# Where the branch to the general path stands in a pooled-attention and mixture-of-experts kernel

## The chip, the cores and the metric

The kernel runs on one core of one Trainium2 chip. The metric is the time of one execution on the device, in microseconds (us); three runs of the kernel before took 638.83, 641.46 and 642.39 us, so the median is 641.46 us. Besides these there is one execution under the hardware profiler.

## What is computed

Attention with pooled keys and values makes 4608 rows of 512 numbers. A gate gives each row a score for each of 8 experts. Scores are taken from the highest down; a row goes to the expert of its best score that still has room (576 rows for each expert). Each expert then applies two matrices to its rows.

```python
def _moe_ref(x, w_gate, w1, w2):
    N, D = x.shape                     # 4608, 512
    E = w_gate.shape[1]                # 8
    cap = N // E                       # 576
    logits = x @ w_gate
    order = np.argsort(-logits.flatten())
    ...
    for idx in order:
        tok, e = int(idx) // E, int(idx) % E
        if assigned[tok] >= 0 or counts[e] >= cap:
            continue
        assigned[tok] = e
        counts[e] += 1
    ...
    for e in range(E):
        mask = assigned == e
        h = np.maximum(x[mask] @ w1[e], 0.0)
        out[mask] = h @ w2[e]
```

`x` is the output of the attention (8 batches, 8 heads, 576 positions, keys and values averaged over 8 neighbours).

## The kernel before

The program has three parts that follow each other. `Attention` works through 36 tiles of 128 rows, writes the rows to memory and collects the gate's scores. `Routing` then closes one expert at a time: a search for the threshold, a list of the 576 rows of this expert. `experts` runs the 8 experts one behind the other while the routing of the next one runs beside it.

An expert has two stages on TensorE (PE). Stage 1 (line 985) multiplies the gathered rows with `w1` in eight pieces of the hidden size, first for 256 columns and then for 320, twelve matmuls for each piece. ScalarE (ACT) applies the ReLU (lines 990, 992) and VectorE (DVE) makes the low part `hl` (line 993). Stage 2 makes five tiles of output. Tiles 0 to 3 take 24 matmuls each (line 1012); tile 4, with the last 64 rows, takes 16 matmuls in the program, which the trace shows as 32 (line 1023). Each tile goes from PSUM to SBUF on ACT (lines 1016, 1028) and from there to its rows in memory by an indirect DMA (a scatter) that GpSimd (POOL) issues (line 999), with a tiny MEMSET of `spacer` ahead of it. PSUM tiles named `h` rotate through five banks, the SBUF tiles `yt` through two.

The fast routing isn't exact in all cases. It adds up in `bad` whatever looks wrong, and `suspect` (lines 792 to 795) makes of it a `flag` by a DVE operation, a matmul with one column and another DVE operation. In the kernel before this stands in stage 2 of the last expert: `suspect` at step 24, and at step 48 each of the five engines loads the flag into a register (line 1225). After the last scatter stands a branch on the flag (line 1058), on every engine; SyncE (SP) only issues DMAs and waits. If the flag is set, `experts_one_by_one` does everything over again with an exact routing, in buffers of its own. If not, a short block follows that raises each engine's semaphores to what they would be after the skipped work: one count for PE, ACT and DVE, nine for SP, and on POOL one count and one instruction that raises the eight semaphores of its DMAs, behind waits for all earlier ones of these DMAs. Then comes the end of the program (line 1319): SP waits for all semaphores, every engine drains and meets the others twice, and POOL clears the semaphores. With the given data the flag isn't set.

The order in which the instructions of one engine stand is made when the program is built: Python generators yield after every matmul, and what is due goes in between. Behind stage 1 of the last expert nothing but stage 2, the branch and the end is left.

Of the kernel before, what the change touches and what calls it, by code (L numbers as in the profile page):

```python
# [883 lines left out]
class Experts:  # L884
# [4 lines left out]
    def __init__(self, tc, wk, psA, xd, w1, w2, out, ident, cap):  # L889
        self.tc, self.nc, self.wk, self.psA = tc, tc.nc, wk, psA  # L890
        self.xd, self.w1, self.w2, self.out, self.ident = xd, w1, w2, out, ident
        self.cap = cap
        self.scatters, self.raw1, self.raw2 = [], [], []
        self.spacer = wk.tile([1, 1], F32, name="spacer", bufs=1)

    @staticmethod
    def part(q):
# [8 lines left out]
    def load_1(self, eid, q0=0, q1=4):  # L906
        nc = self.nc
        r = nc.sync.value_load(eid[0:1, 0:1], min_val=0, max_val=7)
        if q0 == 0:
            self.raw1.append(self.wk.tile([128, 4, 1024], F32, name="raw1", bufs=1))  # L910
        src = self.w1[ds(r, 1)].rearrange("o (j p) f -> p (o j) f", p=128)
        for q in range(q0, q1):
            nc.sync.dma_start(self.raw1[-1][:, *self.part(q)], src[:, *self.part(q)])

    def load_2(self, eid):
        nc = self.nc
        r = nc.sync.value_load(eid[0:1, 0:1], min_val=0, max_val=7)
        raw = self.wk.tile([128, 8, 512], F32, name="raw2", bufs=1)
        src = self.w2[ds(r, 1)].rearrange("o (i p) d -> p (o i) d", p=128)
        for i in range(0, 8, 2):  # L920
            nc.sync.dma_start(raw[:, i:i + 2], src[:, i:i + 2])
        self.raw2.append(raw)

    def gather(self, rows):
        nc = self.nc
        self.xg = self.wk.tile([128, 5, 512], F32, name="xg", bufs=1)
        for t in range(5):
            n = min(128, self.cap - 128 * t)
            nc.gpsimd.indirect_dma_start(out=self.xg[:n, t, :], out_offset=None, in_=self.xd,  # L929
                                         in_offset=bass.IndirectOffsetOnAxis(ap=rows[:n, t:t + 1], axis=0))  # L930

    def high1(self, e, i):
        if i == 0:
            self.w1h = self.wk.tile([128, 4, 1024], F32R, name="w1h", bufs=1)
            self.w1l = self.wk.tile([128, 4, 1024], F32R, name="w1l", bufs=1)
# [6 lines left out]

    def high2(self, e, i):
        if i == 0:
            self.w2h = self.wk.tile([128, 8, 512], F32R, name="w2h", bufs=1)
            self.w2l = self.wk.tile([128, 8, 512], F32R, name="w2l", bufs=1)
        self.nc.scalar.activation(self.w2h[:, i], self.raw2[e][:, i], AF.Copy)

    def low2(self, e, i):
# [2 lines left out]
    def xt(self, t, name="tp", bufs=2, later=lambda after, t, f: f()):  # L952

        nc = self.nc
        n = min(128, self.cap - 128 * t)
        if t == 0:
            self.xh = self.wk.tile([128, 4, 576], F32R, name="xh", bufs=1)
            self.xl = self.wk.tile([128, 4, 576], F32R, name="xl", bufs=1)
# [8 lines left out]
    def stage1(self, later=lambda after, t, f: f(), halves=False):  # L967

        nc = self.nc
        hr = self.wk.tile([128, 8, 64], F32, name="hr", bufs=1)  # L970
        hh = self.wk.tile([128, 8, 576], F32R, name="hh", bufs=1)
        hl = self.wk.tile([128, 8, 576], F32R, name="hl", bufs=1)
        self.hr, self.hh, self.hl = hr, hh, hl
        cols = slice(0, 256), slice(256, 576)
        for o, some in ((cols[0], range(4)), (cols[1], range(4)), (cols[0], range(4, 8)), (cols[1], range(4, 8))) if (
                halves) else ((cols[0], range(8)), (cols[1], range(8))):
            m = o.stop - o.start
            dt = m / 2400 + 0.017
            for f in some:
                ps = self.psA.tile([128, 512], F32, name="h", bufs=5)  # L980
                n = 0
                for a, b in ((self.w1h, self.xh), (self.w1l, self.xh), (self.w1h, self.xl)):
                    for j in range(4):
                        fs = slice(128 * f, 128 * f + 128)
                        nc.tensor.matmul(ps[:, :m], a[:, j, fs], b[:, j, o], start=(n == 0), stop=(n == 11))  # L985
# [4 lines left out]
                nc.scalar.activation(hh[:, f, o], ps[:, :m], AF.Relu)  # L990
                if o.start:
                    nc.scalar.activation(hr[:, f], ps[:, 256:320], AF.Relu)  # L992
                later(0.65, 0.4, lambda f=f, o=o, m=m, ps=ps: nc.vector.scalar_tensor_tensor(  # L993
                    hl[:, f, o], ps[:, :m], 0.0, hh[:, f, o].bitcast(F32), op0=OP.max, op1=OP.subtract))
# [10 lines left out]
    def stage2(self, e, rows, halves):  # L1005
        nc = self.nc
        for t in range(4):
            ps = self.psA.tile([128, 512], F32, name="h", bufs=5)
            o = slice(128 * t, 128 * t + 128)
            for f in range(8):  # L1010
                for k, (a, b) in enumerate(((self.hh, self.w2h), (self.hl, self.w2h), (self.hh, self.w2l))):
                    nc.tensor.matmul(ps, a[:, f, o], b[:, f], start=(f == 0 and k == 0), stop=(f == 7 and k == 2))  # L1012
                    if f < 7 or k < 2:
                        yield 0.2275
            y = self.wk.tile([128, 512], F32, name="yt", bufs=2)
            nc.scalar.activation(y, ps, AF.Copy)  # L1016
            self.scatter(self.out, rows[:, t:t + 1], y)
            yield 0.2275

        ps = self.psA.tile([128, 512], F32, name="h", bufs=5)  # L1020
        for f in range(8):
            for a in range(2):
                nc.tensor.matmul(ps[64 * a:64 * a + 64, :256], self.hr[:, f], self.raw2[e][:, f, 256 * a:256 * a + 256],  # L1023
                                 start=(f == 0), stop=(f == 7))
            if f < 7:
                yield 0.44
        y = self.wk.tile([128, 256], F32, name="yh", bufs=2)
        nc.scalar.activation(y, ps[:, :256], AF.Copy)
        self.scatter(self.out.rearrange("n (a d) -> (n a) d", a=2), halves, y)
        yield 0.44  # L1030


@with_exitstack
def kernel(ctx, tc, q, k, v, wblk, moe_w1, moe_w2, out):
# [23 lines left out]
    with tc.If(flag > 0):  # L1058
# [4 lines left out]
def experts(ctx, tc, g, R, xd, w1, w2, out, ident, cap):  # L1063


    nc = tc.nc
# [129 lines left out]
    for e in range(8):  # L1196
# [5 lines left out]
        for n, dt in enumerate(X.stage1(later, not e)):  # L1202
# [9 lines left out]
                X.load_2(behind(1))  # L1212
            if n >= 64 and n % 2:
                w2.by((n - 70) // 14 if n > 70 else 0)
            advance(min(e + 1, 7), dt)
        while w2.l < 8:
            w2.next()
        w1 = pieces[e + 1] = Pieces(e + 1, X.high1, X.low1)
        for n, dt in enumerate(X.stage2(e, *toks[e])):
            advance(min(e + 1, 7), dt)  # L1220
            if not more and n == 24:
                assert next(g, None) is None
                flag = R.suspect()
            elif not more and n == 48:
                flag = nc.values_load(flag[0:1, 0:1], min_val=0, max_val=1)
            if more and due(e + 1, "id", 9):
                w1.by((n - 60) // 12 if n > 60 else 0)
            if more:
# [8 lines left out]
                turn(e + 1, t)  # L1237
        flush(2)
    flush()
    return flag  # L1240


def experts_one_by_one(ctx, tc, R, xd, w1, w2, out, ident, cap):

    nc = tc.nc
    wk = ctx.enter_context(tc.tile_pool(name="moe2", bufs=2))
    psB = ctx.enter_context(tc.tile_pool(name="psC", bufs=1, space=PSUM))
    X = Experts(tc, wk, psB, xd, w1, w2, out, ident, cap)
    R.restart()
    for e in range(8):  # L1250
        for step in R.exact(e):
# [10 lines left out]
            X.low2(e, i)  # L1262
        for t in range(5):
            X.xt(t)
        for _ in X.stage1():
# [57 lines left out]
```

## Time and profile before

| what | us |
|---|---|
| median of three runs | 641.46 |
| lowest and highest of the three | 638.83, 642.39 |
| the profiled execution, its own time | 640.09 |
| span from its first to its last instruction | 638.2 |
| outside the span, in that execution | 1.9 |
| PE busy in the span | 603.2 (95%) |
| start of the first matmul of stage 2 of the last expert | 598.98 |

The profile gives starts in us from the first instruction of the span. Busy time counts what an engine computes. Waits, branches and register loads belong to the engine's sequencer, which the views mark with a q behind the engine's name (POOLq); they aren't counted as busy, and are listed only by their source line. `PEld` is the loading of weights into PE.

### The profile page before, as it was taken

What the parts mean: (1) busy time and instruction counts of PE and PEld (TensorE: products, weight loads), DVE (VectorE), ACT (ScalarE), POOL (GpSimd) and SP (SyncE); (2) the same over time, 40 slices, a digit from 0 to 9 for tenths busy, and PEclk for the clock granted to TensorE, in tenths of its full rate; (3) what the DMA queues carried; (4) which work ended last, traced back from release to release, by engine and by line L of the source; (5) the groups of instructions that cost most, each with busy time, mean ns of one, the idle gap of its engine ahead of it and who ended that gap; (6) DMA issues with size and microseconds to landing.
All of it is one profiled execution on the core that took longest, in us unless ns stands there. A gap on an engine that the chain in (4) does not pass through costs nothing.

```text
span 638.2 us, 11819 instructions
## 1 busy us (share of the span) xinstructions
PE 603.2 (95%) x4516; PEld 522.3 (82%) x4516; DVE 396.9 (62%) x1142; ACT 244.1 (38%) x561; POOL 174.0 (27%) x215
## 2 busy tenths in 40 slices
PE   6999999994799999999999999999999999999991
PEld 3899998984598789779977987897799889879980
DVE  7677777888886768766862885386378236506100
ACT  6344444442362335233532433252345225415210
POOL 1999996000300410312111302120230213020011
PEclk9799999997799999999999999999999999999996
DMA  9989982121630743308103701630190054013010
GB/s 359 426 333 385 348 311 84 67 83 51 207 134 1 256 157 123 101 34 298 67 17 113 284 1 49 225 139 18 50 339 8 37 207 170 17 64 128 1 51 29
DMA packets 32578, 92.13 MB, mean 144 GB/s; under 512 B 3456, under 2 KB 3456, under 8 KB 29824
## 3 DMA queue, kind: packets, MB, share of 16 engines
q1 hardware_dynamic: 21296, 62.92, 26.5%
q0 software_dynamic: 5888, 18.88, 8.4%
q10 hardware_dynamic: 5328, 9.48, 3.9%
q8 instruction: 37, 0.61, 0.4%
q14 instruction: 29, 0.24, 0.1%
HBM read 72.40 MB, written 18.87 MB: 143 GB/s over the span
## 4 chain that ended last, share of the span: by engine, by line
PE 72%; issue 14%; DVE 7%; POOL 3%; DMA 2%; ACT 1%; POOLq 0%; SPq 0%; ACTq 0%; DVEq 0%
PE h L985 25%; PE h L1012 20%; PE psa L247 7%; PE pss L205 6%; PE h L1023 3%; PE tp L961 2%; PE pse L234 2%; POOL out_dram L999 1%; PE rt L234 1%; PE rt L195 1%; POOL xg L929 1%; PE rt L688 1%; PE rt L605 1%; PE rt L186 1%; PE rt L568 1%
## 5 line engine op out<-in xcount | busy, mean ns | idle before, releaser
L999 POOL DMA_INDIRECT out_dram<-yt,rows x32 | 33.2, 1036 | 280.5 <-ACT yt L1016 280.1
L1012 PE MATMUL h<-w2l,hh 128*128 128x512 f32 x256 | 102.8, 401 | 0.0
L1012 PE MATMUL h<-w2h,hl 128*128 128x512 f32 x256 | 102.0, 399 | 0.0
L1012 PE MATMUL h<-w2h,hh 128*128 128x512 f32 x256 | 101.2, 395 | 0.0
L985 PE MATMUL h<-xl,w1h 128*128 128x320 f32 (+1 forms) x512 | 95.9, 302 | 0.0
L985 PE MATMUL h<-xh,w1h 128*128 128x320 f32 (+1 forms) x512 | 91.2, 299 | 0.7 <-ACT xh L963 0.7
L985 PE MATMUL h<-xh,w1l 128*128 128x320 f32 (+1 forms) x512 | 91.7, 298 | 0.0
L990 ACT ACTIVATE hh<-h 128x320 fp32r<-128x320 f32 (+1 forms) x128 | 51.9, 409 | 99.1 <-PE h L985 96.9
L985 PEld LDWEIGHTS h<-xh,w1h 128*128 128x128 f32 x512 | 75.3, 189 | 3.6 <-issue 2.7
L985 PEld LDWEIGHTS h<-xl,w1h 128*128 128x128 f32 x512 | 77.0, 190 | 0.7
L985 PEld LDWEIGHTS h<-xh,w1l 128*128 128x128 f32 x512 | 76.1, 189 | 0.2
L965 DVE TENSOR_TENSOR xl<-tp,xh 128x512 fp32r<-128x512 f32 (+1 forms) x40 | 25.3, 633 | 78.7 <-ACT xh L963 78.4
L993 DVE SCALAR_TENSOR_TENSOR hl<-h,hh 128x320 fp32r<-128x320 f32 (+1 forms) x128 | 57.4, 451 | 25.3 <-ACT hr L992 16.3
L929 POOL DMA_INDIRECT xg<-xd,rows x40 | 39.7, 992 | 96.6 <-DVE rows L699 62.9
L1016 ACT ACTIVATE yt<-h 128x512 f32<-128x512 f32 x32 | 19.1, 597 | 119.7 <-PE h L1012 103.8
L247 PE MATMUL psa<-vblk,eT 128*128 128x146 f32 (+3 forms) x400 | 61.9, 303 | 0.0
L1012 PEld LDWEIGHTS h<-w2h,hl 128*128 128x128 f32 x256 | 48.1, 188 | 9.0
L1012 PEld LDWEIGHTS h<-w2l,hh 128*128 128x128 f32 x256 | 48.4, 189 | 8.2
L1012 PEld LDWEIGHTS h<-w2h,hh 128*128 128x128 f32 x256 | 48.2, 188 | 8.3
L247 PEld LDWEIGHTS psa<-vblk,eT 128*128 128x128 f32 (+1 forms) x400 | 52.2, 181 | 1.7 <-DVE xt L272 0.3
L205 PE MATMUL pss<-kblk,rawq 128*128 128x144 f32 (+1 forms) x320 | 45.9, 302 | 3.6 <-DVE e L216 2.8
L941 DVE TENSOR_TENSOR w1l<-raw,w1h 128x512 fp32r<-128x512 f32 x64 | 41.2, 686 | 8.1 <-ACT w1h L937 7.9
(194 smaller groups left out, 905.4 us busy)
## 6 DMA issues: line engine op xcount, KB each, us to landing
raw<-in_moe_w_dram SPq DMA_DIRECT2D x64, 512.0 KB, 6.8
xd<-xt ACTq DMA_DIRECT2D x36, 256.0 KB, 4.3
rawv<-in_v_dram SPq DMA_DIRECT2D x7, 1280.0 KB, 11.5
rawk<-in_k_dram SPq DMA_DIRECT2D x7, 1152.0 KB, 8.1
rawq<-in_q_dram SPq DMA_DIRECT2D x7, 1152.0 KB, 13.5
rawk<-in_k_dram SPq DMA_DIRECT2D x2, 576.0 KB, 4.6
rawv<-in_v_dram SPq DMA_DIRECT2D x1, 768.0 KB, 7.2
rawq<-in_q_dram SPq DMA_DIRECT2D x1, 640.0 KB, 8.7
```

The lines of the kernel that those rows point to most:

```text
L205: nc.tensor.matmul(ps[cols, j // 2, 144 * (j % 2):144 * (j % 2) + 144], self.q_of(b, j, n, cols.stop - cols.start), self.kblk[b % 4][:, j] ...
L234: nc.tensor.transpose(ps[:127, 128 * m:128 * m + 128], self.e[i][:, o:o + 127], self.ident)
L247: self.nc.tensor.matmul(o[h], self.eT[i][:, c, h], self.vblk[b % 4][:, self.BLOCKS[c]:self.BLOCKS[c + 1]], start=(c == cs[0]), stop=(c == ...
L929: nc.gpsimd.indirect_dma_start(out=self.xg[:n, t, :], out_offset=None, in_=self.xd, in_offset=bass.IndirectOffsetOnAxis(ap=rows[:n, t:t + ...
L941: self.nc.vector.tensor_tensor(l, raw, h.bitcast(F32), op=OP.subtract)
L965: later(1.3, 0.65, lambda: nc.vector.tensor_tensor(xl, ps[:, :, :n], xh, op=OP.subtract))
L985: nc.tensor.matmul(ps[:, :m], a[:, j, fs], b[:, j, o], start=(n == 0), stop=(n == 11))
L990: nc.scalar.activation(hh[:, f, o], ps[:, :m], AF.Relu)
L993: later(0.65, 0.4, lambda f=f, o=o, m=m, ps=ps: nc.vector.scalar_tensor_tensor(hl[:, f, o], ps[:, :m], 0.0, hh[:, f, o].bitcast(F32), op0= ...
L999: st = nc.gpsimd.indirect_dma_start(out=rows, out_offset=bass.IndirectOffsetOnAxis(ap=idx, axis=0), in_=y, in_offset=None)
L1012: nc.tensor.matmul(ps, a[:, f, o], b[:, f], start=(f == 0 and k == 0), stop=(f == 7 and k == 2))
L1023: nc.tensor.matmul(ps[64 * a:64 * a + 64, :256], self.hr[:, f], self.raw2[e][:, f, 256 * a:256 * a + 256], start=(f == 0), stop=(f == 7))
```

## The change

The branch moves from behind the last scatter to behind the products of the last expert's tile 1. Ahead of it stand now stage 1, tile 0 with its scatter, and the 24 matmuls of tile 1, whose sums stay in a PSUM bank. The branch follows. Behind it, for both paths, tile 1 is copied out and scattered and the tiles 2 to 4 are made. The general path therefore works in the same buffers as the fast one (`buf`, `fixed`) with two other PSUM banks (`bank`), and leaves out these last parts. The rows of the last expert are copied into `lastrows` (`keep`) so that both paths find them at one place. `suspect` and the load of the flag move into stage 1 of the last expert (steps 48 and 136).

```diff
-        flag = experts(c2, tc, g, R, xd, moe_w1, moe_w2, out, A.ident, cap)
-    with tc.If(flag > 0):
-        with ExitStack() as c2:
-            experts_one_by_one(c2, tc, R, xd, moe_w1, moe_w2, out, A.ident, cap)
+        rows = cst.tile([128, 6], I32, name="lastrows")
+        def keep():
+            nc.vector.tensor_copy(rows[:, :5], R.rows)
+            nc.vector.tensor_copy(rows[:, 5:], R.halves)
+        X, flag, ps = experts(c2, tc, g, R, xd, moe_w1, moe_w2, out, A.ident, cap, keep)
+        fast, X.scatters, X.fixed = X.scatters, [], True
+        with tc.If(flag > 0):
+            experts_one_by_one(X, R, ps)
+            keep()
+        X.scatters += fast
+        X.put(1, ps, rows, rows[:, 5:])
+        for _ in X.stage2(7, rows, rows[:, 5:], range(2, 5)):
+            pass
...
+            if not more and n == 48:
+                assert next(g, None) is None
+                flag = R.suspect()
+                keep()
+            elif not more and n == 136:
+                flag = nc.values_load(flag[0:1, 0:1], min_val=0, max_val=1)
             advance(min(e + 1, 7), dt)
...
-        for n, dt in enumerate(X.stage2(e, *toks[e])):
+        for n, dt in enumerate(X.stage2(e, *toks[e], range(5 if more else 1))):
             advance(min(e + 1, 7), dt)
-            if not more and n == 24:
-                assert next(g, None) is None
-                flag = R.suspect()
-            elif not more and n == 48:
-                flag = nc.values_load(flag[0:1, 0:1], min_val=0, max_val=1)
...
-    return flag
+    ps = psB.tile([128, 512], F32, name="h", bufs=5)
+    for _ in X.products(7, 1, ps):
+        pass
+    return X, flag, ps
...
+    def buf(self, name, shape, dtype=F32):
+        if not self.fixed:
+            self.bufs[name] = self.wk.tile(shape, dtype, name=name, bufs=1)
+        return self.bufs[name]
...
-        for _ in X.stage2(e, R.rows, R.halves):
+        for _ in X.stage2(e, R.rows, R.halves, range(5 if e < 7 else 1), bank):
             pass
+    for _ in X.products(7, 1, ps):
+        pass
```

`stage2` is split into `products` (the matmuls of a tile) and `put` (the copy and the scatter), which do what its body did before.

On PE, at the branch, the kernel before has the following; `hr` and `raw` belong to tile 4, and a name in brackets is the semaphore of an engine or a DMA that is waited for.

```order
L1012 MATMUL h<-w2l,hh 128x512
L1023 MATMUL h<-raw_7185,hr 64x256 [waits DMAHW4_49,Activation_49]
L1023 MATMUL h<-raw_7185,hr 64x256 x3
L1023 MATMUL h<-raw_7185,hr 64x256 [waits DMAHW5_49]
L1023 MATMUL h<-raw_7185,hr 64x256 x3
L1023 MATMUL h<-raw_7185,hr 64x256 [waits DMAHW6_49]
L1023 MATMUL h<-raw_7185,hr 64x256 x3
L1023 MATMUL h<-raw_7185,hr 64x256 [waits DMAHW7_49]
L1023 MATMUL h<-raw_7185,hr 64x256 x3
L1058 COMPARE_AND_BRANCH
```

On PE, where the two paths meet again in the changed kernel: the first row is the last matmul of the general path, the first branch leaves it, the second ends the short block of the fast path (its count waits for PE itself), and tile 2 follows.

```order
L1026 MATMUL h<-w2l,hh 128x512
L1081 UNCONDITIONAL_BRANCH
L1081 UNCONDITIONAL_BRANCH [waits PE_49]
L1026 MATMUL h<-w2h,hh 128x512 [waits DVE_49,Activation_49]
L1026 MATMUL h<-w2h,hl 128x512 [waits DVE_49]
L1026 MATMUL h<-w2l,hh 128x512
L1026 MATMUL h<-w2h,hh 128x512 [waits Activation_49]
```

Tile 4 stood ahead of the branch; now 64 matmuls of the program (tiles 2, 3 and 4) stand behind it, and the first of them stands behind a wait of PE for its own tile 1.

On POOL, at the branch, before: the scatters of tiles 1 to 4 stand ahead of it.

```order
L998 MEMSET spacer 1x1 [waits Pool_49]
L999 DMA out_dram<-yt,rows 4608x512 [waits DMASW5_49,Activation_49]
L998 MEMSET spacer 1x1 [waits Pool_49]
L999 DMA out_dram<-yt,rows 4608x512 [waits DMASW6_49,Activation_49]
L998 MEMSET spacer 1x1 [waits Pool_49]
L999 DMA out_dram<-yh,halves 9216x256 [waits DMASW7_49,DVE_49,Activation_49]
L1058 COMPARE_AND_BRANCH
```

On POOL, behind the branch, in the changed kernel: the row ISA is the instruction that raises the semaphores of the DMAs.

```order
L1081 UNCONDITIONAL_BRANCH
L1081 ISA [waits Pool_49,DMASW4_49,DMASW5_49,DMASW3_49,DMASW6_49,DMASW2_49,DMASW7_49,DMASW1_49,DMASW0_49]
L1081 UNCONDITIONAL_BRANCH
L1005 MEMSET spacer 1x1 [waits Pool_49]
L1006 DMA out_dram<-yt,lastrows 4608x512 [waits DMASW4_49,DVE_49,Activation_49]
L1005 MEMSET spacer 1x1 [waits Pool_49]
L1006 DMA out_dram<-yt,lastrows 4608x512 [waits DMASW5_49,Activation_49]
L1005 MEMSET spacer 1x1 [waits Pool_49]
L1006 DMA out_dram<-yt,lastrows 4608x512 [waits DMASW6_49,Activation_49]
L1005 MEMSET spacer 1x1 [waits Pool_49]
L1006 DMA out_dram<-yh,lastrows 9216x256 [waits DMASW7_49,DVE_49,Activation_49]
L1351 UNCONDITIONAL_BRANCH
```

Four scatters that stood ahead of this instruction now stand behind it, and between the last scatter and the end of the program stands nothing any more.

On ACT the copies of tiles 1 to 4 stand behind the branch, and the first of them waits for the semaphores of five DMAs of POOL.

```order
L1081 UNCONDITIONAL_BRANCH
L1081 UNCONDITIONAL_BRANCH [waits Activation_49]
L1040 ACTIVATE yt<-h 128x512 [waits DMASW3_49,DMASW2_49,DMASW4_49,DMASW0_49,DMASW6_49,PE_49,Activation_49]
L1040 ACTIVATE yt<-h 128x512 [waits DMASW3_49,DMASW5_49,DMASW1_49,DMASW7_49,PE_49,Activation_49]
L1040 ACTIVATE yt<-h 128x512 [waits DMASW4_49,PE_49,Activation_49]
L1044 ACTIVATE yh<-h 128x256 [waits PE_49]
```

Ahead of stage 1 of the last expert, all engines do the same in the same order as before.

More of the change, by code (lines that the diff above doesn't have):

```diff
@@ L925, in gather @@
         nc = self.nc
[L926 removed]
+        self.xg = self.buf("xg", [128, 5, 512])
         for t in range(5):
@@ L944, in high2 @@
         if i == 0:
-            self.w2h = self.wk.tile([128, 8, 512], F32R, name="w2h", bufs=1)
-            self.w2l = self.wk.tile([128, 8, 512], F32R, name="w2l", bufs=1)
+            self.w2h = self.buf("w2h", [128, 8, 512], F32R)
+            self.w2l = self.buf("w2l", [128, 8, 512], F32R)
         self.nc.scalar.activation(self.w2h[:, i], self.raw2[e][:, i], AF.Copy)
@@ L965, in xt, with stage1 @@
         later(1.3, 0.65, lambda: nc.vector.tensor_tensor(xl, ps[:, :, :n], xh, op=OP.subtract))
-    def stage1(self, later=lambda after, t, f: f(), halves=False):
+    def stage1(self, later=lambda after, t, f: f(), halves=False, bank=("h", 5)):
         nc = self.nc
-        hr = self.wk.tile([128, 8, 64], F32, name="hr", bufs=1)
-        hh = self.wk.tile([128, 8, 576], F32R, name="hh", bufs=1)
-        hl = self.wk.tile([128, 8, 576], F32R, name="hl", bufs=1)
+        hr = self.buf("hr", [128, 8, 64])
+        hh = self.buf("hh", [128, 8, 576], F32R)
+        hl = self.buf("hl", [128, 8, 576], F32R)
         self.hr, self.hh, self.hl = hr, hh, hl
@@ L979, in stage1 @@
             for f in some:
-                ps = self.psA.tile([128, 512], F32, name="h", bufs=5)
+                ps = self.psA.tile([128, 512], F32, name=bank[0], bufs=bank[1])
                 n = 0
@@ L1003, in scatter, with stage2, products @@
         self.scatters.append(st)
-    def stage2(self, e, rows, halves):
+    def stage2(self, e, rows, halves, parts=range(5), bank=("h", 5)):
+        for t in parts:
+            ps = self.psA.tile([128, 512], F32, name=bank[0], bufs=bank[1])
+            yield from self.products(e, t, ps)
+            self.put(t, ps, rows, halves)
+            yield 0.2275 if t < 4 else 0.44
+    def products(self, e, t, ps):
         nc = self.nc
[L1007 to L1010, printed above, removed]
+        o = slice(128 * t, 128 * t + 128)
+        for f in range(8):
+            if t < 4:
                 for k, (a, b) in enumerate(((self.hh, self.w2h), (self.hl, self.w2h), (self.hh, self.w2l))):
@@ L1014, in stage2, with put @@
                         yield 0.2275
+            else:
+                for a in range(2):
+                    nc.tensor.matmul(ps[64 * a:64 * a + 64, :256], self.hr[:, f],
+                                     self.raw2[e][:, f, 256 * a:256 * a + 256], start=(f == 0), stop=(f == 7))
+                if f < 7:
+                    yield 0.44
+    def put(self, t, ps, rows, halves):
+        if t < 4:
             y = self.wk.tile([128, 512], F32, name="yt", bufs=2)
-            nc.scalar.activation(y, ps, AF.Copy)
+            self.nc.scalar.activation(y, ps, AF.Copy)
             self.scatter(self.out, rows[:, t:t + 1], y)
[L1018 to L1030, printed above, removed]
+        else:
+            y = self.wk.tile([128, 256], F32, name="yh", bufs=2)
+            self.nc.scalar.activation(y, ps[:, :256], AF.Copy)
+            self.scatter(self.out.rearrange("n (a d) -> (n a) d", a=2), halves, y)
 @with_exitstack
```

25 lines of the change are left out of this document (12 added, 13 removed).

## Prediction

> **What bounds the kernel now.** First the page, for the span and the chain of work that ended last.
>
> ```profile
> span 638.2 us, 11819 instructions
> PE 72%; issue 14%; DVE 7%; POOL 3%; DMA 2%; ACT 1%; POOLq 0%; SPq 0%; ACTq 0%; DVEq 0%
> ```
>
> PE sets the pace nearly everywhere, and the edit touches PE only in the last expert. So the timeline of its last matmuls comes next, then the busy times of stretches behind them.
>
> ```profile
> 620.89 0.39 PE L1012 MATMUL h<-w2l,hh 128*128 128x512 f32 x1
> 621.21 3.67 PE L1023 MATMUL h<-raw,hr 128*64 128x256 f32 x32
> 624.93 0.38 ACT L1028 ACTIVATE yh<-h 128x256 f32<-128x256 f32 x1 [2.97 <-PE h L1023]
> 625.59 0.97 POOL L999 DMA_INDIRECT out_dram<-yh,halves  x1 [2.29 <-ACT yh L1028]
> ...
> 630.80:637.40 6.60, 0.00 (x0) 0.00 (x0) 0.00 (x0) 0.00 (x0) 0.00 (x0) 0.50 0.00 0
> 637.40:638.20 0.80, 0.00 (x0) 0.00 (x0) 0.00 (x0) 0.00 (x0) 0.00 (x0) 0.50 0.00 0
> ```
>
> PE is through at 621.21 + 3.67 = 624.9, the last scatter is issued by 626.6, and yet the span goes on to 638.2 with no engine computing and no DMA moving in its last 7.4 us. What happens there stands under the lines of the branch (1058) and of the program's end (1319), with the DMA view for the time that a scatter takes to land.
>
> ```profile
> L1058 SPq EVENT_SEMAPHORE  x9: 17/17/17, 608.3 to 608.9; - x9
> L1058 POOLq EVENT_SEMAPHORE  x5: 17/43/43, 628.0 to 628.9; - x5
> L1058 SPq COMPARE_BRANCH  x1: 53/53/53, 605.7 to 605.7; - x1
> L1058 PEldq COMPARE_BRANCH  x1: 3395/3395/3395, 622.6 to 622.6; - x1
> L1058 ACTq COMPARE_BRANCH  x1: 50/50/50, 624.9 to 624.9; - x1
> L1058 POOLq COMPARE_BRANCH  x1: 53/53/53, 625.4 to 625.4; - x1
> L1058 PEldq EVENT_SEMAPHORE  x1: 51/51/51, 626.0 to 626.0; - x1
> L1058 ACTq EVENT_SEMAPHORE  x1: 17/17/17, 627.5 to 627.5; - x1
> L1058 POOLq INC_SWDGE_SEM  x1: 1788/1788/1788, 628.9 to 628.9; - x1
> ...
> L1319 SPq EVENT_SEMAPHORE  x14: 17/28/28, 630.7 to 638.1; - x14
> L1319 POOLq DRAIN  x3: 40/107/6600, 630.8 to 637.9; - x3
> L1319 SPq DRAIN  x3: 7/7/13, 631.4 to 637.6; - x3
> ...
> out_dram<-yt,rows POOLq DMA_INDIRECT x4, 2.9
> out_dram<-yh,halves POOLq DMA_INDIRECT x1, 3.2
> ```
>
> Read as a chain: the last scatter lands at 625.59 + 3.2 = 628.8; POOL's waits for landed DMAs end there (628.9). INC_SWDGE_SEM, which raises the semaphores for the skipped DMAs, takes 1.79 us, to 630.7. POOL's first drain then takes 6.60 us, to 637.4, and the engines' last meeting 0.8. SP's twelve waits begin at 630.7 and its drains at 631.4, so SP is done 6 us before POOL. What bounds the end is the landing, the increments and the drain, in a row. The page's chain doesn't show it, since it ends with the last instruction that computes.
>
> **What goes from the end.** With the branch behind tile 1, the increments and the wait for their own scatter come four scatters earlier. Behind the last landing there remain SP's waits and the meeting: at most 631.4 - 630.7 = 0.7 us (the last scatter is the fourth of the twelve waits, so rather 0.5) and 0.8 us. The end would stand at 628.8 + 0.7 + 0.8 = 630.3 in place of 638.2: **7.9 us less**, as long as POOL's drain is short there. The same row's other two drains took 0.107 and 0.040 us; the long one is the one right behind INC_SWDGE_SEM. So I take the 6.6 us as work of that instruction which POOL finishes behind its record. The bounds of the drain at the new end are 0.04 and 6.60 us; I choose the lower, for the following rows.
>
> ```profile
> 605.56 0.97 POOL L999 DMA_INDIRECT out_dram<-yt,rows  x1 [31.44 <-ACT yt L1016]
> 606.53 0.09 POOL L998 MEMSET spacer<- 1x1 f32 x1
> ```
>
> The MEMSET starts when the scatter's 0.97 us are over: POOL has nothing left of a scatter after its record.
>
> **What the jump costs on PE.** Each engine that takes the branch is silent for some time: SP 605.7 to 608.3 (2.6 us), ACT 624.9 to 627.5 (2.6), POOL 625.4 to 628.0 (2.6), PE 622.6 to 626.0 (3.4, here inside the branch's own record). The DMA view tells what it waits for, in a window behind SP's and DVE's branches and one behind PE's:
>
> ```profile
> q14 instruction: 2, 0.02, 2.9%
> ...
> q8 instruction: 1, 0.02, 5.4%
> ```
>
> Two instruction pages in 1.75 us of 16 DMA engines (2.9%) are 0.4 us each; PE's single one in 1.1 us (5.4%) is 0.95 us. PE's jump is longer by about that difference, so its 3.4 us are a fetch, and not a wait for its matmuls, which ended at 624.9. The cover is PE's queue: the sequencer runs ahead of the array.
>
> ```profile
> L1023 PEldq EVENT_SEMAPHORE  x1: 51/51/51, 617.1 to 617.1; - x1
> 610.01 0.39 PE L1012 MATMUL h<-w2l,hh 128*128 128x512 f32 x1
> 610.24 0.39 PE L1012 MATMUL h<-w2h,hh 128*128 128x512 f32 x1
> 610.49 0.60 ACT L1016 ACTIVATE yt<-h 128x512 f32<-128x512 f32 x1 [5.20 <-PE h L1012]
> 598.83 0.19 PEld L1012 LDWEIGHTS h<-w2h,hh 128*128 128x128 f32 x1
> 598.98 0.39 PE L1012 MATMUL h<-w2h,hh 128*128 128x512 f32 x1
> ```
>
> The wait ahead of tile 4 was handled at 617.1, while the matmul just ahead of it started at 620.89: 3.8 us ahead, 17 matmuls of 0.23 us (610.24 - 610.01). Behind tile 1 stand the same matmuls, so the branch is taken 3.8 us before the last of them starts, and the 3.4 us fit in with 0.4 to spare. If that cover were gone, the jump would cost its 3.4 us. What stays open is the short block's wait for PE's own last product: the queue runs dry. From the start of the last matmul of tile 1 to the first of tile 2 I count 0.39 (the matmul), 0.09 (until its semaphore is seen: ACT starts 0.09 behind 610.01 + 0.39), two waits of 0.05, and 0.15 from weight load to matmul (598.83 to 598.98), less some overlap: 0.68. Normal is 0.23, so the **stall is 0.45 us**. Its bounds are 0.1 (620.89 to 621.21 at the change to tile 4, less 0.23) and 3.9 (the jump exposed, plus this).
>
> The Trainium skill bears on this, in "Runtime: NRT & Kernel Launch", section "Instruction fetch mechanics": a taken branch whose target isn't in the current two pages waits for a DMA that fetches the page, which speaks against a branch in the middle of PE's work. By that rule of the Trainium skill alone the sum would lose the whole jump, as in the second case of rival 1 below. The trace agrees that there is a fetch; that it lies behind queued matmuls is what the rows above add.
>
> **What is moved and added besides.** The flag's matmul had this price in stage 2:
>
> ```profile
> 604.44 0.39 PE L1012 MATMUL h<-w2h,hh 128*128 128x512 f32 x1
> 604.76 0.16 PE L794 MATMUL rt<-ones,rc 128*1 128x1 bf16 x1
> 605.19 0.40 PE L1012 MATMUL h<-w2l,hh 128*128 128x512 f32 x1
> ```
>
> From 604.44 to 605.19 one matmul of 0.23 lies between two, 0.75 for 0.46: it cost 0.3 us. In stage 1 it costs the like, so its move is 0, between -0.3 and +0.3. The loads of the flag stand in every engine's sequencer before and after; with PE's queue ahead they cost nothing. DVE gets two tiny copies and makes the flag ahead of one `hl`:
>
> ```profile
> 579.75 0.42 DVE L993 SCALAR_TENSOR_TENSOR hl<-h,hh 128x256 fp32r<-128x256 f32 x1 [1.02 <-ACT hh L990]
> 584.89 0.75 PE L985 MATMUL h<-xh,w1h 128*128 128x320 f32 x4
> ```
>
> DVE idles 1.02 us ahead of it. Waiting for the flag's matmul may push it back by some 0.4 us; its PSUM bank is next wanted, five banks on, at 584.89. That is 4.7 us of cover, so 0. Without it, each `hl` would hold PE by what it is late.
>
> The waits behind the branch need the scatters of tiles 1 and 2:
>
> ```profile
> 611.36 0.97 POOL L999 DMA_INDIRECT out_dram<-yt,rows  x1 [4.74 <-ACT yt L1016]
> 616.80 0.97 POOL L999 DMA_INDIRECT out_dram<-yt,rows  x1 [4.38 <-ACT yt L1016]
> ```
>
> Tile 0's scatter lands at 605.56 + 2.9 = 608.5, so the increments run from 608.5 to 610.3, hidden by tile 1's products. ACT's copy of tile 1 waits for them and for PE, as before at 610.5. On POOL, the 6.6 us behind the increments hold back tile 1's scatter until 610.3 + 6.6 = 616.9 in place of 611.4; behind it are queued tile 2's (ready at 616.8) and, one tile of 5.4 us later, tile 3's. Each takes 1.06 us with its MEMSET, so POOL is level again by 619.0. ACT's copy of tile 3 reuses tile 1's SBUF tile, which is free at 616.9 + 0.1 + 2.9 = 619.9, and wants it at 620.89 + 0.39 + 0.09 = 621.4. Both hide it, with 1.5 us to spare at least. Other engines have jumped by 608 and hold nobody.
>
> Sum: -7.9 + 0.45 + 0 = **-7.4 us**. The profiled execution took 640.09, span 638.2 and 1.9 around it; with the same 1.9 it becomes 632.7. It lies 1.4 below the median of the three runs and 0.6 below the mean of all four executions, 640.7, which I take as the level: **633.3**.
>
> **Rivals.**
> 1. *PE drains before it jumps on.* In the trace PE resumes at 626.0, 1.1 us behind its last matmul, and that could be a rule. For: no row shows a fetch that ended while matmuls were queued. Against: the lengths of the fetches above. The stall would be 0.39 + 1.1 + 0.3 - 0.23 = 1.6: -6.3, 634.4. With no cover at all it would be 3.9: -4.0, 636.7.
> 2. *The long drain belongs to the end*, whatever stands ahead of it, so the change doesn't bring what it says. For: one case only, at the end. Against: the MEMSET right behind the scatter, and no DMA was left to wait for. POOL then drains from 626.6 + 0.45 = 627.0 to 633.6, and 0.8: -3.8, 636.9.
> 3. *Slower: the 6.6 us move from the drain to each scatter behind the increments*, at POOL's queue (its state would have to be made good with every later DMA). The last issue would start at 610.3 + 4 x 6.6 + 3 x 1.06 = 639.9, and the end be at 639.9 + 3.2 + 1.5 = 644.6: +6.4, 647.1. It decides from 5.0 us a scatter (equal) and 5.8 (over 0.5%). Against: 0.97 us is a scatter's price everywhere in the trace, but no row shows one behind the increments.
>
> **How the numbers follow.** Forecast 0.70, rival 1 with 1.1 us 0.10, exposed 0.04, rival 2 0.12, rival 3 0.04. A measurement here tells 0.5%, 3.2 us, from no change. The forecast and rival 1 lie beyond it; rival 2, 3.8 below the level, falls inside half of the time. Faster 0.90, within 0.06, slower 0.04. The lower end: no stall (632.8) less 1.5 for the spread of executions (638.83 to 642.39): 631.3. The upper reaches rival 2 and the exposed jump: 637.2.
>
> **What would show it.** Right: a start-to-start gap near 0.7 us on PE between tiles 1 and 2; INC_SWDGE_SEM near 608.5; POOL's first drain at the end under 0.2 us; tile 1's scatter late, near 617; the span 630.8. A PE gap of 1.8 or 4 us is rival 1, a 6.6 us drain at the end rival 2, scatters 6 us apart rival 3. Wrong it would also be if something in stage 1 of the last expert came later by over 1 us.

## The result, and the profile after

The changed kernel takes **634.61 us**, the median of 14 executions (632.74 to 638.40), beside 640.74 of the kernel before (14 executions, 638.06 to 642.39). The ratio is 0.9924, with a 95% interval of 0.9901 to 0.9946: 4.9 us less, between 3.5 and 6.3. The forecast was 633.3 (631.3 to 637.2), and faster by over 0.5%. A second set of 12 executions gave 634.67 and 0.9923 (0.9893 to 0.9953). The time is near the forecast, but the profile shows that the main step of the forecast was wrong. The profiled execution took 637.23 us, with a span of 635.4; it is one of the longer of the 14.

First the timeline of the changed kernel's end, the counterpart of the rows of before that begin at 620.89 (start, duration, engine, line, operation).

```profile
622.31 0.39 PE L1026 MATMUL h<-w2l,hh 128*128 128x512 f32 x1
...
622.62 3.67 PE L1031 MATMUL h<-raw,hr 128*64 128x256 f32 x32
...
626.35 0.38 ACT L1044 ACTIVATE yh<-h 128x256 f32<-128x256 f32 x1 [2.97 <-PE h L1031]
627.00 0.97 POOL L1006 DMA_INDIRECT out_dram<-yh,lastrows  x1 [2.29 <-ACT yh L1044]
```

Then the stretches behind it (busy time of PE, PEld, DVE, ACT and POOL, then the clock, the DMA share and GB/s).

```profile
628.00:629.40 1.40, 0.00 (x0) 0.00 (x0) 0.00 (x0) 0.00 (x0) 0.00 (x0) 1.00 0.26 94
629.50:634.60 5.10, 0.00 (x0) 0.00 (x0) 0.00 (x0) 0.00 (x0) 0.00 (x0) 0.66 0.00 0
634.60:635.40 0.80, 0.00 (x0) 0.00 (x0) 0.00 (x0) 0.00 (x0) 0.00 (x0) 0.50 0.00 0
```

The last scatter has landed by 629.4, and there are still 5.1 us in which nothing computes and nothing moves. The instructions of the branch (line 1081 now) and of the program's end (1351) say who fills them: each row has count, shortest/median/longest in ns, and the start of the first and of the last.

```profile
L1081 POOLq EVENT_SEMAPHORE  x5: 17/43/1647, 609.2 to 611.1; - x5
L1081 SPq COMPARE_BRANCH  x1: 53/53/53, 581.2 to 581.2; - x1
L1081 DVEq COMPARE_BRANCH  x1: 72/72/72, 601.0 to 601.0; - x1
...
L1081 ACTq COMPARE_BRANCH  x1: 50/50/50, 605.9 to 605.9; - x1
L1081 POOLq COMPARE_BRANCH  x1: 53/53/53, 606.5 to 606.5; - x1
L1081 PEldq COMPARE_BRANCH  x1: 3942/3942/3942, 607.0 to 607.0; - x1
L1081 ACTq EVENT_SEMAPHORE  x1: 17/17/17, 608.5 to 608.5; - x1
L1081 POOLq INC_SWDGE_SEM  x1: 1708/1708/1708, 611.2 to 611.2; - x1
L1081 PEldq EVENT_SEMAPHORE  x1: 51/51/51, 611.3 to 611.3; - x1
...
L1351 POOLq DRAIN  x3: 40/113/7813, 626.8 to 635.2; - x3
L1351 SPq DRAIN  x3: 7/7/13, 630.0 to 634.9; - x3
```

The increments left the end, as meant: they run at 611.2 to 612.9. SP drains from 630.0, 0.6 us behind the landing. But **POOL's first drain is still there**. It is on record from 626.8, when POOL's sequencer reached it behind the last issue, and ends at 626.8 + 7.8 = 634.6: 6.6 us behind the end of the scatter's record at 627.0 + 0.97. In the kernel before it took 6.60 us directly behind the increments. From the start of the last scatter's issue to the end of the span there were 638.2 - 625.59 = 12.6 us; there are 635.4 - 627.00 = 8.4 now, where the forecast had 4.7.

In the middle of stage 2 the new wait looks as follows, on PE, POOL and ACT.

```profile
610.85 0.39 PE L1026 MATMUL h<-w2l,hh 128*128 128x512 f32 x1
611.53 0.47 PE L1026 MATMUL h<-w2h,hh 128*128 128x512 f32 x1 [0.30 <-PEq L1081]
...
612.98 0.09 POOL L1005 MEMSET spacer<- 1x1 f32 x1 [5.26 <-DMA out_dram<-yt,rows]
...
613.04 0.60 ACT L1040 ACTIVATE yt<-h 128x512 f32<-128x512 f32 x1 [6.57 <-DMA out_dram<-yt,rows]
...
613.92 0.97 POOL L1006 DMA_INDIRECT out_dram<-yt,lastrows  x1 [0.85 <-ACT yt L1040]
```

From the last matmul of tile 1 to the first of tile 2 are 0.68 us. POOL's MEMSET follows the increments at once, at 612.98, and tile 1's scatter starts at 613.92, not near 617.

### The profile page after: what moved, and what is told of

Its sections match the earlier page's. It is cut to its first block, busy times and chain, and to the rows that moved or that the text cites. A ratio compares the mean times of both kernels' runs of the same rounds, so it can differ in the third digit from the quotient of the medians.

```text
span 635.4 us, 11825 instructions
## 1 busy us (share of the span) xinstructions
PE 605.0 (95%) x4516; PEld 524.1 (82%) x4516; DVE 394.5 (62%) x1144; ACT 244.1 (38%) x561; POOL 174.8 (28%) x215
## 4 chain that ended last, share of the span: by engine, by line
issue 47%; PE 24%; POOL 14%; DMA 9%; DVE 4%; ACT 0%; POOLq 0%; SPq 0%; DVEq 0%; ACTq 0%
DMA out_dram<-yt,rows 7%; PE psa L247 6%; POOL xg L936 6%; POOL out_dram L1006 6%; PE pss L205 5%; PE h L992 5%; PE h L1026 2%; PE pse L234 2%; PE rt L234 1%; PE rt L195 1%; PE rt L186 1%; PE rt L568 1%; DMA rawk<-in_k_dram 1%; DMA xg<-xd,rows 1%; DMA raw<-in_moe_w_dram 1%
## 5 line engine op out<-in xcount | busy, mean ns | idle before, releaser
L1006 POOL DMA_INDIRECT out_dram<-yt,rows x29 | 30.3, 1046 | 262.1 <-ACT yt L1040 261.6
```

What stands on the lines that cost most here:

```text
L1006: st = nc.gpsimd.indirect_dma_start(out=rows, out_offset=bass.IndirectOffsetOnAxis(ap=idx, axis=0), in_=y, in_offset=None)
```

## The experiments

Software DMAs are here the gathers and scatters that POOL issues, 40 of each. Three theories stood at first. *A, a debt*: POOL's drain makes good something for each software DMA issued since the drain before, so it can be paid early. *B* and *C*: it has a fixed price, B at any drain, C at the program's end. Against all of them stood the forecast's own reason, that the time hangs on the increments.

**A drain in POOL's idle time** (mid_drain), a line in the loop over stage 1:

```diff
+            elif not more and n == 100:
+                nc.gpsimd.drain()
             elif not more and n == 136:
                 flag = nc.values_load(flag[0:1, 0:1], min_val=0, max_val=1)
```

> The changed kernel with one drain of POOL added in stage 1 of the last expert (n = 100), where POOL idles for some 20 us. 75 of the 80 software DMAs (40 gathers, 40 scatters) are ahead of it, 5 behind. Theory A, a debt: POOL's drain makes good something for every software DMA since the drain before, 6.6 / 80 = 0.083 us each. Then the added drain takes 6.2 us in POOL's idle time, the first one at the end 0.4 us; the end is set by the last scatter's landing and SP's waits, span 4.5 us shorter than the changed kernel's, time 630.1. Theory B, a fixed price of any drain behind POOL's DMAs: both take 6.6 us, time 634.6. Theory C, it belongs to the program's end: the added one under 0.2 us, the end's 6.6, time 634.6.

Measured: 629.10 us, ratio to before 0.9827 (0.9795 to 0.9859). The rows of the end, of the increments and of the added drain (line 1248):

```profile
L1353 POOLq DRAIN  x3: 46/113/2899, 623.0 to 626.8; - x3
L1353 SPq DRAIN  x3: 7/7/13, 626.2 to 626.5; - x3
...
L1081 POOLq INC_SWDGE_SEM  x1: 203/203/203, 607.3 to 607.3; - x1
...
L1248 POOLq DRAIN  x1: 9169/9169/9169, 570.0 to 570.0; - x1
```

and POOL's timeline around both drains:

```profile
570.19 0.97 POOL L1006 DMA_INDIRECT out_dram<-yh,halves  x1 [2.29 <-ACT yh L1044]
579.78 0.09 POOL L1005 MEMSET spacer<- 1x1 f32 x1 [8.62 <-issue]
...
623.22 0.97 POOL L1006 DMA_INDIRECT out_dram<-yh,lastrows  x1 [2.29 <-ACT yh L1044]
```

The added drain ends at 579.2, 8.0 us behind the issue ahead of it, while PE computes. The one at the end is over 1.7 us behind the last issue (623.0 + 2.9 = 625.9), and SP's drains at 626.2 end last. B and C are out; of A's numbers neither fits closely (6.2 and 0.4 us were expected, 8.0 and 1.7 measured). The increments, of which no expectation had spoken, shrank too: 0.20 us in place of 1.71.

**The same drain with the branch in its old place** (old_place_drain): the kernel before with the two added lines.

> The kernel before, with its branch at the end, and the same added drain in stage 1 of the last expert. It separates the drain from the branch's place. Theory A (debt): end drain 0.4 us, SP's waits and drains then end last, some 0.7 us behind the increments; span 638.2 - 6.6 + 0.7 = 632.3, time 634.8, as fast as the changed kernel without the branch moved. Theories B and C: no change, 640.7, end drain 6.6 us.

Measured: 633.79 us, ratio 0.9877 (0.9852 to 0.9903). This added drain alone is worth no less than the whole change.

```profile
L1321 POOLq DRAIN  x3: 46/107/463, 630.8 to 632.1; - x3
...
L1058 POOLq INC_SWDGE_SEM  x1: 288/288/288, 630.5 to 630.5; - x1
```

A long drain isn't tied to the increments ahead of it, nor to the program's end: here it stands right behind them and takes 0.46 us.

**The change without its branch** (no_branch):

```diff
-        with tc.If(flag > 0):
-            experts_one_by_one(X, R, ps)
-            keep()
```

> The changed kernel without its branch: the general path for tied or odd inputs is left out, as is the increment of the skipped DMAs' semaphores; the flag is still made and loaded. It shows what the branch still costs in its new place. If the jump is covered by PE's queue: the start-to-start gap of PE between tiles 1 and 2 falls from 0.68 us to 0.23-0.3, tile 4 ends 0.4 us earlier, POOL's end drain stays 6.6 us whatever the increments did (theories A, B and C alike). If the long drain hangs on the increments (my forecast's reason): end drain under 0.2 us and a span 4.9 us shorter than the changed kernel's.

Measured, in the rows of the end and on PE between tiles 1 and 2:

```profile
L1348 POOLq DRAIN  x3: 40/113/7813, 625.8 to 634.2; - x3
```

```profile
610.43 0.39 PE L1026 MATMUL h<-w2l,hh 128*128 128x512 f32 x1
610.66 0.39 PE L1026 MATMUL h<-w2h,hh 128*128 128x512 f32 x1
```

With no increments at all the drain is 7813 ns, to the nanosecond that of the changed kernel. And the start-to-start gap is 0.23 us: the branch costs PE 0.68 - 0.23 = 0.45 in its new place. By the end drain the forecast's own reason is out. The single time, 636.20, tells nothing at this size.

**How does the debt grow?** Five kernels vary the number of software DMAs since the last drain. eight_drains has the added line in every expert (`if n == 100:`), drain_expert3 and drain_expert1 in one (`if e == 3 and n == 100:` and 1). few_scatters adds none and leaves out the scatters of the first seven experts, and so their rows of the output:

```diff
-            self.put(t, ps, rows, halves)
+            self.put(t, ps, rows, halves, e == 7)
...
+            if out:
+                self.scatter(self.out, rows[:, t:t + 1], y)
```

drain_first is the kernel before with a drain ahead of its first gather.

> The changed kernel with a POOL drain in stage 1 of each of the eight experts (n = 100). Software DMAs ahead of each since the drain before: 5, 10, 10, 10, 10, 10, 10, 10, and 5 for the one at the end. Theory A (debt per DMA): 0.4, then seven times 0.8, end 0.4 us. Theory B (fixed): nine times 6.6 us. Theory C: eight times under 0.2, end 6.6. A debt that grows with POOL's other instructions (most of them in the first 110 us) rather than with its DMAs: the first long, the others short.

> The changed kernel with one added POOL drain, in stage 1 of the fourth expert: 40 software DMAs ahead of it, 40 behind. Theory A (debt per DMA, 6.61 / 80 = 0.083 us): the first drain at the end finishes 40 x 0.083 = 3.3 us behind the end of the last scatter's issue; if the debt is added to the 1.69 us that five DMAs left, it is 1.69 + 35 x (6.61 - 1.69) / 75 = 4.0. INC_SWDGE_SEM took 1.71 us with 76 DMAs since the last drain and 0.20 with one, so with 36 near 0.9. Theory D (only the first drain of a program is dear, as a code that must be brought in once): 1.69 us at the end as with the drain in the last expert, INC_SWDGE_SEM 0.2.

> The same with the drain in stage 1 of the second expert: 15 software DMAs ahead, 65 behind. Theory A: 65 x 0.083 = 5.4 us behind the end of the last scatter's issue (5.6 if added to the 1.69), INC_SWDGE_SEM 1.4 us with 61. Theory D: 1.69 and 0.2 us.

> The changed kernel without the scatters (and their MEMSETs) of the first seven experts; their rows of the output are left out. No drain is added; 45 software DMAs are left, 40 gathers and 5 scatters. Theory A (debt per DMA): end drain 45 x 0.083 = 3.7 us behind the end of the last issue (4.3 if added to 1.69), INC_SWDGE_SEM with 41 of them 1.0 us, in place of 1.71. Theory D or a debt in time or in POOL's other work: 6.6 us. A debt of scatters alone: 1.69 us; of gathers alone: 6.6 us.

> The kernel before, with a POOL drain ahead of its first software DMA: some 90 of POOL's own instructions ahead of it, no software DMA. Theory A (debt per DMA): it takes under 0.2 us, INC_SWDGE_SEM 1.8 and the first drain at the end 6.6 us as before; from the start of the last scatter to the span's end 12.6 us; time 640.7, ratio 1.000. A debt of POOL's other work would show here as a long drain. It is also the control for the runs' gains, which came out larger than what the ends of the traces account for (-4.9 for -3.7 us with the change, -11.1 for -8.2 with the drain in the last expert): if each build has an offset of its own, whatever is changed in it, the ratio here lies 0.2 to 0.4% away from 1.

Two of them in the rows of their ends, first drain_expert3 and then few_scatters, each with the last scatter from its timeline:

```profile
L1353 POOLq DRAIN  x3: 46/113/4543, 625.1 to 630.3; - x3
...
L1081 POOLq INC_SWDGE_SEM  x1: 908/908/908, 609.3 to 609.3; - x1
```

```profile
625.38 0.97 POOL L1006 DMA_INDIRECT out_dram<-yh,lastrows  x1 [2.29 <-ACT yh L1044]
```

```profile
L1353 POOLq DRAIN  x3: 40/113/4955, 623.8 to 629.3; - x3
...
L1083 POOLq INC_SWDGE_SEM  x1: 1004/1004/1004, 608.2 to 608.2; - x1
```

```profile
624.02 0.97 POOL L1006 DMA_INDIRECT out_dram<-yh,lastrows  x1 [2.29 <-ACT yh L1045]
```

The drain of drain_expert3 ends at 625.1 + 4.54 = 629.6, 3.3 us behind the end of the last issue; that of few_scatters 3.8 behind. The four kernels of this group that ran on the changed one took 631.07 (eight_drains), 632.34 (drain_expert3), 632.68 (drain_expert1) and 631.37 us (few_scatters) in one execution each, which is too few to order them. All kernels together, with branch_stage1 from below (the column "0.083 n" is 6.61 / 80 for each DMA, and 0.19 + 0.02 n a line through the increments of old_place_drain and of the kernel before; nothing else is fitted; tail runs from the start of the last scatter's issue to the end of the span):

| kernel | DMAs since the last drain, n | 0.083 n | end drain, behind the last issue | DMAs at the increments | 0.19 + 0.02 n | increments | tail |
|---|---|---|---|---|---|---|---|
| after | 80 | 6.6 | 6.6 | 76 | 1.71 | 1.71 | 8.4 |
| no_branch | 80 | 6.6 | 6.6 | none | - | - | 8.4 |
| branch_stage1 | 80 | 6.6 | 6.6 | 75 | 1.69 | 1.69 | 8.4 |
| drain_expert1 | 65 | 5.4 | 5.4 | 61 | 1.41 | 1.41 | 7.2 |
| few_scatters | 45 | 3.7 | 3.8 | 41 | 1.01 | 1.00 | 5.6 |
| drain_expert3 | 40 | 3.3 | 3.3 | 36 | 0.91 | 0.91 | 5.1 |
| mid_drain, eight_drains | 5 | 0.4 | 1.7 | 1 | 0.21 | 0.20 | 3.9 |
| before | 80 | 6.6 | 6.60, behind the increments | 80 | 1.79 | 1.79 | 12.6 |
| drain_first | 80 | 6.6 | 6.60, behind the increments | 80 | 1.79 | 1.79 | 13.4 |
| old_place_drain | 5 | 0.4 | 0.46, behind the increments | 5 | 0.29 | 0.29 | 6.0 |

At the program's end the debt per DMA holds at each n from 40 on, so theory D (only the first drain is dear), which gave 1.69 us wherever a drain had gone ahead, is out. It holds for gathers (few_scatters leaves 40 of them) as for scatters. The increments have a debt too: 0.02 us for each DMA. The increments don't pay the drain's, since after and no_branch have the same drain. Counted by rows in place of DMAs (each expert's fifth gather has 64 rows, all the others and the scatters 128), few_scatters would have 3.6 and 0.96 us; it has 3.75 and 1.00, where DMAs give 3.72 and 1.01. Bytes aren't told apart from DMAs. With n = 5 it is not the debt that counts: in mid_drain the last packet of the last scatter ends at 625.3 in the trace, and the drain 0.6 us behind it.

The added drains in the middle don't follow the formula. Those of eight_drains took 6.25 to 10.96 us as recorded, and end 2.7 to 6.4 us behind the issue ahead of them, where 5 to 15 DMAs each (the expectation had 5 or 10; the trace has 15 ahead of the third) would make 0.4 to 1.2. In the trace each ends 0.7 to 1.1 us behind the last packet of POOL's DMAs, which land late there: with few DMAs the drain waits for their landing. Behind the last packet it is 1.0 us with 15 DMAs (drain_expert1), 2.1 with 40 (drain_expert3) and 3.4 to 3.6 with 75 (mid_drain, mid_drain_again, old_place_drain; 8.0 to 8.5 behind the issue, where 6.2 are due). So it grows with the DMAs there too, but by another rule, which is not settled; it was hidden in idle time of POOL. In drain_first the drain ahead of the first DMA is over 0.07 us behind POOL's last TensorTensor, with some 90 instructions of POOL ahead of it:

```profile
104.83 1.66 POOL L176 TENSOR_TENSOR vblk<-vsum,mask 128x128 f32<-128x128 f32 x3
```

```profile
L1173 POOLq DRAIN  x1: 1756/1756/1756, 104.8 to 104.8; - x1
...
L1320 POOLq DRAIN  x3: 40/107/6600, 631.2 to 638.4; - x3
```

104.8 + 1.756 is 106.6, and the work of line 176 ends at 104.83 + 1.66 = 106.5: there is no debt of other work, and the increments and the end drain are as before. Its tail isn't the 12.6 us expected but 13.4, because the last scatter took 4.1 us to land in place of 3.2. This kernel's time is 640.91, ratio 1.0015 (0.9990 to 1.0040).

**What covers PE's jump** (branch_stage1): the branch two tiles earlier, behind stage 1.

```diff
-        for n, dt in enumerate(X.stage2(e, *toks[e], range(5 if more else 1))):
+        for n, dt in enumerate(X.stage2(e, *toks[e], range(5 if more else 0))):
...
-        X.put(1, ps, rows, rows[:, 5:])
-        for _ in X.stage2(7, rows, rows[:, 5:], range(2, 5)):
+        for _ in X.stage2(7, rows, rows[:, 5:]):
             pass
```

> The changed kernel with its branch behind stage 1 of the last expert; all five tiles of stage 2 follow it. PE's queue there holds 17 matmuls of 0.147 us, 2.5 us, in place of 17 of 0.227, 3.8 us. If the queue is what covers the jump (3.4 to 3.9 us by PE's branch rows): PE's silence, from the start of the last matmul of stage 1 to the first of stage 2, is 3.4-3.9 - 2.5 + 0.6 = 1.5 to 2.0 us, against 0.68 behind tile 1; span 1 us longer than the changed kernel's. If a jump's fetch is always hidden: 0.6 to 0.7 us. If PE drains before it jumps on: over 3.5 us.

Measured: 642.01 in a single execution, span 640.1, which is too few to rank it; by the trace it is some 1 us slower than the kernel before (PE's last expert takes 5.2 us more, the tail 4.2 less). The timeline of PE, then the stretches:

```profile
599.55 0.75 PE L992 MATMUL h<-xl,w1h 128*128 128x320 f32 x4
603.16 0.49 PE L1026 MATMUL h<-w2h,hh 128*128 128x512 f32 x1 [2.87 <-ACTq L1081]
604.01 0.80 PE L1026 MATMUL h<-w2h,hl 128*128 128x512 f32 x1 [0.35 <-DVEq L1081]
604.61 0.63 PE L1026 MATMUL h<-w2l,hh 128*128 128x512 f32 x1
605.03 0.63 PE L1026 MATMUL h<-w2h,hh 128*128 128x512 f32 x1
```

```profile
603.80:607.20 3.40, 3.19 (x8) 2.52 (x9) 0.00 (x0) 0.00 (x0) 0.00 (x0) 0.50 0.01 5
607.30:612.00 4.70, 4.70 (x22) 3.84 (x21) 0.00 (x0) 0.60 (x1) 0.01 (x1) 1.00 0.00 0
```

And the branch's rows:

```profile
L1081 PEldq COMPARE_BRANCH  x1: 3746/3746/3746, 597.5 to 597.5; - x1
L1081 ACTq COMPARE_BRANCH  x1: 50/50/50, 600.3 to 600.3; - x1
L1081 DVEq COMPARE_BRANCH  x1: 72/72/72, 600.9 to 600.9; - x1
L1081 ACTq EVENT_SEMAPHORE  x1: 17/17/17, 603.1 to 603.1; - x1
L1081 DVEq EVENT_SEMAPHORE  x1: 21/21/21, 603.9 to 603.9; - x1
```

My expectation failed, on engines that I had left out. PE's own part came as the queue theory has it: its branch is on record from 597.5 for 3.75 us, so PE was back at 601.3, 1.3 us behind the start of its last matmul (the last of the four from 599.55, at 599.99). But PE then waited for ACT until 603.1 and for DVE until 604.0. Both reach the branch only when the last piece of stage 1 is copied, and then jump for 2.8 and 3.0 us. So from start to start PE is silent for 603.16 - 599.99 = 3.17 us. Just behind it the granted clock fell to 0.50, from 603.8 to 607.2, with matmuls 0.42 apart in place of 0.23: from 604.01 to 607.43 there are 8 of them, 3.4 us in place of 1.8, so 1.6 lost. Behind tile 1 ACT and DVE jump at 605.9 and 601.0, while PE still computes tile 1. That place is cheap for their sake as much as for PE's.

**The comparison once more.** On one chip, the changed kernel and mid_drain beside it:

> The changed kernel once more, to set it beside the next run on one chip. By the end of its trace -4.2, PE's stall and the flag +0.5: ratio 0.994; by its first 14 executions 0.9924.

> The changed kernel with the POOL drain in stage 1 of the last expert once more. By the end of its trace -8.7 + 0.5 = -8.2 against the kernel before: ratio 0.987; by its first six executions 0.983. Against the changed kernel beside it: 4.5 us less by the traces, 5.5 by the first runs.

Measured: 634.67, ratio 0.9923 (0.9893 to 0.9953), and 631.25, ratio 0.9866 (0.9830 to 0.9903). The drain in the last expert is the faster kernel of the two again; its gain over before is 8.6 us by the ratio, close to what its trace accounts for (8.2: the tail 12.6 - 3.9 = 8.7 less, PE 0.5 more, as worked out below).

## Why the prediction was right and wrong, step by step

- **The drain: the step that failed.** "So I take the 6.6 us as work of that instruction which POOL finishes behind its record." It isn't: no_branch has no such instruction and the same drain. Of the bounds 0.04 and 6.60 us I took the lower, and the upper one was true. My reason was the MEMSET that starts when a scatter's 0.97 us are over. The row is right, but it shows only that POOL can begin its next work; what a drain will ask for later doesn't show in it. Two readings of the one long drain stood against each other, that it comes from the increments and, as rival 2, that it belongs to the end, and I gave the second 0.12. Neither is the answer, which was in the number of DMAs ahead of it; a single trace doesn't vary that. In the sum the term of the end was -7.9 and is 12.6 - 8.4 = 4.2 us less.
- **The sum that fits the trace is rival 2's**, 3.8 us less, though not its reason: in old_place_drain the drain at the end takes 0.46 us. By the traces the tail lost 4.2 us and PE took 0.5 back: its last expert, up to the start of the last matmul, is that much longer (the stall 0.45, the matmuls right behind the stall 0.1, and moving the flag's matmul nothing, as forecast). That makes 3.7. The 14 executions say 4.9 (3.5 to 6.3), which includes it.
- **The landing and the increments** did leave the end, and SP's waits fit: 0.6 us behind the landing, forecast at most 0.7. The 1.79 us of the increments is itself mostly a debt of 80 DMAs and no fixed price.
- **PE's stall** was right, mechanism and size: 0.68 us from start to start, 0.45 above the normal 0.23. PE's branch ends at 607.0 + 3.9 = 610.9, when the last matmul of tile 1 starts (610.85). So the rival in which PE drains ahead of its jump is out, and so is an exposed jump. What is left is the wait for PE's own last product: in after_again the branch ends 0.4 us ahead of the start of that matmul and in eight_drains 0.3 us behind it, and the gap is 0.68 and 0.69 all the same. On the rule of the Trainium skill that a taken branch waits for a fetch ("Runtime: NRT & Kernel Launch", "Instruction fetch mechanics"): the wait of 3.9 us is there, behind queued matmuls.
- **The increments' place** was wrong without harm. I had them at 608.5 to 610.3, they ran at 611.2 to 612.9, because POOL had to jump first (606.5 to 609.2) and tile 0's scatter landed only at 611.0 (issued at 606.76, 4.2 us to land in place of 2.9). ACT's copy of tile 1 waited for them until 613.04, where PE's product alone would have let it start at 610.85 + 0.39 + 0.09 = 611.3. The PSUM bank of tile 1 isn't wanted again, so nobody waited for that.
- **The scatters behind the branch** came on time, since no 6.6 us lay between. That also ends rival 3, the slower one: the debt isn't charged to later DMAs.
- **The time was near the forecast by luck.** The measured 634.61 lies 1.3 us from the forecast and 2.3 from rival 2, whose sum the trace bears out; and the range reached up to rival 2. Both comparisons gained 1.2 us more than the 3.7 of the traces. Their intervals include 3.7, so nothing has to be explained by that. The control drain_first came out at 1.0015, so a changed line need not make a gain of its own. Executions differ by up to 4 us ahead of the last expert, in work that the change doesn't touch: mid_drain's profiled one was 3.8 us ahead of before's at its 200th matmul, at 40 us, the changed kernel's 0.9 ahead there and 1.0 behind after 190 us. In that stretch the granted clock was halved for longer in the changed kernel's profile (the first row) than in that of the kernel before (the second):

```profile
146.50:173.70 27.20, 17.06 (x198) 12.89 (x198) 19.84 (x82) 6.01 (x15) 5.51 (x6) 0.50 0.42 138
150.00:167.00 17.00, 9.32 (x134) 5.88 (x133) 13.10 (x55) 3.23 (x6) 3.82 (x4) 0.50 0.33 97
```

What sets the length of these stretches stays open.

## What to carry to other kernels

Before a term is put down to the instruction that stands next to it, ask what else in the program it could count: here the drain was a bill for 80 DMAs issued over 460 us, and a drain added in an idle stretch of POOL pays it early (631.25 and 629.10 us in place of 634.6). A branch in the middle of the work is cheap where every engine that the next product waits for has reached it early: PE's is covered by its queue (what is left, 0.45 us, is the wait for its own last product), but behind the last piece of a stage the jumps of ACT and DVE are bare, and 3 us of silence cost another 1.6 us in the clock. And a forecast that lands in its range isn't yet an explained one: the tail's terms tell which mechanism was at work.

## What the runs showed of the hardware

- POOL's first drain at the program's end finishes 0.083 us for each software DMA since the drain before behind POOL's last instruction (6.6 us for 80, 3.3 for 40), whether increments stand ahead of it or not, and with 5 of them 0.6 us behind the last packet (mid_drain). INC_SWDGE_SEM costs 0.19 us and 0.02 for each DMA. Neither shows at the DMAs themselves: an issue stays at 0.97 us. The Trainium skill ("VectorE: DVE Perf Modes", "The DRAIN you can't avoid") speaks of drains that the runtime puts at a program's start and end, as about 12 ns, constant, on all engines. The drains here stand under a line of the kernel; SP's (7 to 13 ns) are as short, POOL's first one (6600 ns) isn't.
- In branch_stage1 the granted clock fell to 0.50 for 3.4 us behind a silence of PE of 3.2 us from start to start (2.87 us idle), with matmuls of 512 columns 0.42 us apart. The Trainium skill ("TensorE: Matmul & The Clock Gate", sections "What's actually happening" and "Wait — 56ns, not 53.3ns?") has 426.7 ns for them on a cold array, which agrees, and halves the clock after an idle window of some 3.4 us; PE's idle time here was a little shorter.
- The span follows the mean granted clock from execution to execution: among the changed kernel's 14, 630.9 us at 0.983 and 636.6 at 0.967.
